# Counting ranks: column sums of compare tables on TensorE in place of later compares on VectorE

## The chip, the cores and the metric

The kernel runs on one core of a Trainium2 chip. The metric is the device time of one execution in microseconds, as the median of several runs. A hardware profile of one further execution gives the page and the trace that are read here. The engines are TensorE (PE, with its weight loads as PEld), VectorE (DVE), ScalarE (ACT), GpSimd (POOL) and SyncE (SP), which issues most of the DMAs. Each engine works through its own queue in order, and semaphores tie the queues together.

## What is computed

The program is a linear attention followed by a mixture-of-depths expert layer. For 4 batches, 8 heads, 768 positions and head size 64, the attention goes through blocks of 64 positions with a decaying state:

```python
for b in range(nb):
    intra = np.einsum('bhic,bhjc->bhij', qb, kb) * Dmask[None]
    intra = np.einsum('bhij,bhjd->bhid', intra, vb)
    inter = np.einsum('bhid,bhde->bhie', qb * lam_pow[None], kv_state)
    out[:, :, sl] = intra + inter
    kv_state = lam_block[None, :, None, None] * kv_state + np.einsum('bhsd,bhse->bhde', kb_dec, vb)
```

Its output, with heads side by side, is x of shape (4, 768, 512). In the second part each batch chooses the 128 positions with the highest gate score, and only these pass through a two-layer network:

```python
scores = np.einsum('bsd,d->bs', x, w_gate)
for b in range(B):
    top_idx = np.argpartition(-scores[b], capacity)[:capacity]
    xe = x[b, top_idx]
    ye = np.maximum(xe @ w1, 0.0) @ w2
    g = 1.0 / (1.0 + np.exp(-scores[b, top_idx]))
    out[b, top_idx] = x[b, top_idx] + g[:, None] * ye
```

## The kernel before

**Tiling and steps.** Positions are taken in groups of 128, two blocks of 64 each. A batch has NT = 6 groups, and the whole input NG = 24. The main loop has one step per group g. A step finishes group g and prepares the next ones: it multiplies masked scores by the values (`from_scores`, L356), copies the result out of PSUM to `x_b` on ScalarE (`outputs`, L370 and L372), starts the score products of group g+1 (`scores`, L285, and `from_states`, L345), masks them on VectorE (`masked`, L292), and for group g+2 computes the state products (`state_products`, L308), transposes queries and keys (`transposes`, L219 and L233, or `split_transposes`, L257, late in the run; ScalarE copies them to `qkT`), and decays queries on GpSimd (`queries_decayed`, L270). Keys are decayed on GpSimd (`keys_decayed`, L205). The state is advanced by `decay_state` on GpSimd (L318) and `next_state` on VectorE (L335), or by four folded operations on VectorE alone (L330).

**Order.** The schedule is manual: each engine gets its instructions in the order in which the Python calls are made. Steps below SPARE = 6 have one order, step SPARE has a mixture, and later steps have another. Work of the experts is put into later steps as numbered pieces (`put(step, key, piece)`, sorted by key by `in_order`), or into the dictionaries `front`, `early`, `gates`, `ranked` and `writes`.

**Ranks.** The gate score of each position is a product of `x_b` and the gate weights on VectorE (`gate_scores`, L395). To find the 128 best positions, the kernel counts for each position how many others beat it. One step after its group, `row` (L418) makes TensorE transpose the group's scores into a PSUM bank so that they lie along a row on every partition. ScalarE copies this to `sc_row` (L421), and VectorE compares it with the group's own scores, for ties (L424). `compare` (L434) then compares all scores of the groups up to this one with the group's own scores, one position per partition, and adds up the hits along the row into `beaten`. Comparing with groups that come later has to wait until these exist. `count_later` does that: in step t = 2, 4 and 5 of a batch (more of it in the last batch) it runs further compares (also L434) of older groups against newer parts of the row. `compare_older` takes a part of the last group's compare before the row is there. When a batch is counted, `ranks` adds the counts (L470) and builds a 0/1 table `hit` (L475). `tokens` multiplies it by position numbers on TensorE (`pk`, L486) and VectorE makes the list `tok` (L492, L495). With it GpSimd fetches the chosen rows (`xs`, L509). The expert transposes them (`pt`, L519), computes `ph` (L547) and `py` (L561), combines (`y`, L569), and GpSimd writes rows back (L577).

**Banks and loads.** Two PSUM banks, pm0 and pm1, are handed out in turn by `bank()` for `tq`, `tk`, `tqk`, `pb`, `pk`, `pt`; `ph` and `py` hold one over several steps. A bank's next user waits for the readers of the one before. The state products and, from step SPARE on, the transposed keys share one bank for each of the two blocks (`pu`). Loads of q, k and v go through pools of seven buffers, three loads are under way at a time, and the variable `ahead` says how many groups in advance they are asked for (4, then 3, then 5).

Of the kernel before, what the change touches and what calls it, by code (L numbers as in the profile page):

```python
# [9 lines left out]
BF16 = mybir.dt.bfloat16  # L10
I32 = mybir.dt.int32
AF = mybir.ActivationFunctionType
# [5 lines left out]
def kernel(  # L18
# [12 lines left out]
    nc = tc.nc  # L31
# [68 lines left out]
    def load_weights(i):  # L100
# [10 lines left out]
            src[j * 128 : (j + n) * 128, cols].rearrange("(c p) e -> p c e", p=128),  # L111
        )

    ident = const.tile([128, 128], FP32, name="ident")
    make_identity(nc, ident)

# [221 lines left out]
    def from_states(g):  # L338

        qs = qss.pop(g)  # L340
        for hp, hh, c in quarters():
            n = 2 * g + c
            if n % (2 * NT) == 0:
                continue
            nc.tensor.matmul(  # L345
                pos[g][half[hh ^ c], hh, 0, hp, :],
                lhsT=qs[half[hh], c, hp, :], rhs=states[n][half[hh], hp, :],
                start=(hp == 0), stop=False, skip_group_check=True,
            )
        for c in range(2):  # L350
            states.pop(2 * g + c, None)

    def from_scores(g):
        p, vn = ps_.pop(g), loaded.pop(g)[2]
# [47 lines left out]

        return out[0 : b + 1].flatten_outer_dims()

    rows_, beatens, toks, upto = {}, {}, {}, {}

    def row(g, pb=None):

        b, t = divmod(g, NT)
        if t == 0:  # L410
            rows_[b] = mod.tile([128, S], FP32, name="sc_row", tag="sc_row")
            beatens[b] = mod.tile([128, NT, NT + 1], FP32, name="beaten")
            nc.vector.memset(beatens[b][:], 0.0)
            upto[b] = {n: n for n in range(NT)}
        if pb is None:
            pb = bank([128, L], "pb")
        pb = pb[:, :L]
        nc.tensor.transpose(  # L418
            pb, in_=scs[b][:, t : t + 1].broadcast_to([128, 128]), identity=ident[:]
        )  # L420
# [3 lines left out]
        nc.vector.scalar_tensor_tensor(  # L424
            out=cmp[:, :L], in0=pb, scalar=scs[b][:, t : t + 1], in1=not_before[:],
            op0=ALU.is_equal, op1=ALU.mult, accum_out=beatens[b][:, t, NT : NT + 1],
        )

    def count(b, t, cols, op, at):
        cmp = mod.tile([128, S], BF16, name="cmp")
        nc.vector.tensor_scalar(  # L434
            out=cmp[:, : cols.stop - cols.start], in0=rows_[b][:, cols],
            scalar1=scs[b][:, t : t + 1], scalar2=None, op0=op, op1=ALU.add,
            accum_out=beatens[b][:, t, at : at + 1],
        )

    def count_later(b, groups, last):  # L440
        for t in groups:
            if upto[b][t] < last:
                cols = slice((upto[b][t] + 1) * L, (last + 1) * L)
                count(b, t, cols, ALU.is_gt, last)
                upto[b][t] = last

    def compare(g):
        b, t = divmod(g, NT)
        first = upto[b].pop(NT + t, 0)
        count(b, t, slice(first * L, (t + 1) * L), ALU.is_ge, t)  # L450
        if t == NT // 2 - 1 or t == NT - 1 or (b == B - 1 and t == NT - 2):
            count_later(b, range(t), t)
        elif t == NT - 2:
            count_later(b, range(NT // 3), t)

    def compare_older(g):

        b, t = divmod(g, NT)
        if t > 0:
            count(b, t, slice(0, t * L), ALU.is_ge, 0)  # L460
            upto[b][NT + t] = t

    def places(b):

# [125 lines left out]
    def put(step, key, piece):  # L590
        later.setdefault(step, []).append((key, piece))
# [5 lines left out]
    def plan(b):  # L597
        last = b == B - 1
        s = (b + 1) * NT
        ranks, tokens = places(b)  # L600
        if last:

            def last_row():
                compare_older(NG - 1)
                row(NG - 1, us[NG][1])
                compare(NG - 1)
                ranks()

            put(s, 35, last_row)
            put(s, 85, tokens)  # L610
        else:

            if b > 0:
                ranked[s + 1] = ranks
                if s + 8 <= NG:
                    put(s + 2, 1, tokens)
                else:
                    early.setdefault(s + 2, []).append(tokens)
            else:
                put(s, 1, ranks)  # L620
# [77 lines left out]
    for g in range(NG):  # L698
        if g == NT:
            for i, at in enumerate(weights_at):  # L700
                if at == g:
                    load_weights(i)
        ahead = 4 if g < NT - 1 else 3 if g < NT + 4 else 5
        while asked < min(g + ahead + 1, NG):
            load(asked)
            asked += 1
        if g != NT:
            for i, at in enumerate(weights_at):
                if at == g:
# [6 lines left out]
        if spare:  # L716
# [17 lines left out]
            state_products(g + 2)  # L734
            next_state(2 * g + 4)
            gate_scores(g)
            next_state(2 * g + 5, fold=True)
        else:
            lead = g > SPARE
            if g == SPARE:  # L740

                for r in rows:
                    row(r)
            if g + 2 < NG:
                if g <= FED:
                    keys_decayed(g + 2)
                decay_state(2 * g + 4)
            if FED <= g < NG - 3:
                keys_decayed(g + 3)
            from_scores(g)  # L750
            outputs(g)
            if g + 1 < NG:
                scores(g + 1)
                from_states(g + 1)
                if g == SPARE:
                    for r in rows:
                        compare(r)
                    in_order(pieces)
                masked(g + 1)
            if g % NT == 0 and lead and NGR:  # L760
                compare_older(g - 1)
            for piece in early.pop(g, []):
# [10 lines left out]
            if g in gates:  # L773
                gates.pop(g)()
            if g + 2 < NG:
                if g > SPARE + 1:
# [10 lines left out]
                in_order(pieces)  # L787
            if lead:
                for r in rows:
                    row(r, us[NG][0] if r == NG - 2 else None)  # L790
            if g + 2 < NG:
                next_state(2 * g + 5, fold=not lead)
            if lead:
# [43 lines left out]
```

## Time and profile before

The time before is 184.74 us (median of 3 runs, 183.54 to 185.18). The profiled execution has a span of 180.2 us.

| engine | busy us | share of the span | instructions |
|---|---|---|---|
| PE | 149.8 | 83% | 3586 |
| PEld | 119.5 | 66% | 3586 |
| DVE | 111.5 | 62% | 378 |
| ACT | 68.9 | 38% | 178 |
| POOL | 96.2 | 53% | 100 |

Busy time is an average over stages with different limits, so the chain of waits and the windows must say where an engine's time matters. A row of the page's groups reads: source line, engine, operation, output and inputs with shapes, count, busy time and mean duration of one, then the idle time of the engine just ahead of these instructions and what ended it. The DMA queues moved 31.99 MB in all and were nearly full until about 126 us.

### The profile page before, as it was taken

The numbers are of one execution on the slowest core, as the hardware profiler recorded it, in microseconds if no ns is written. First come the engines' busy times: TensorE is split into PE (matmuls) and PEld (weight loads), VectorE is DVE, ScalarE is ACT, GpSimd is POOL, SyncE is SP. The second block draws the span as 40 slices with busy tenths as digits, with TensorE's granted clock in tenths as the row PEclk, the third lists the DMA queues.
The fourth block names the chain that finished last, engine by engine and source line by source line (L and its number), as shares of the span: only waits on it lengthen the run. The fifth ranks groups of instructions, "written<-read, shape, count | busy, mean of one in ns | idle before, by whom it ended". The sixth has DMA issues, their size and how long they took to land.

```text
span 180.2 us, 8244 instructions
## 1 busy us (share of the span) xinstructions
PE 149.8 (83%) x3586; PEld 119.5 (66%) x3586; DVE 111.5 (62%) x378; ACT 68.9 (38%) x178; POOL 96.2 (53%) x100
## 2 busy tenths in 40 slices
PE   0799777776497999999977989989999997989980
PEld 0568666665386999776655668977666896459620
DVE  4814788899844445768996583589865779330010
ACT  2214555562144344644552552563343641011100
POOL 4358666945074665569786967867574600220002
PEclk9999999999859999999999999999999999999997
DMA  4999798999999998987999999989112131011001
GB/s 97 205 226 219 195 261 221 235 276 307 289 248 272 208 275 180 199 181 174 262 242 290 225 253 245 256 215 238 62 64 62 62 125 50 7 55 58 0 0 58
DMA packets 83381, 31.99 MB, mean 177 GB/s; under 512 B 75665, under 2 KB 79761, under 8 KB 83346
## 3 DMA queue, kind: packets, MB, share of 16 engines
q1 hardware_dynamic: 82560, 29.37, 67.8%
q0 software_dynamic: 640, 2.10, 3.4%
q8 instruction: 28, 0.46, 1.1%
q14 instruction: 7, 0.06, 0.1%
q10 hardware_dynamic: 146, 0.01, 0.0%
HBM read 24.12 MB, written 7.34 MB: 175 GB/s over the span
## 4 chain that ended last, share of the span: by engine, by line
PE 55%; issue 16%; DVE 14%; POOL 6%; DMA 4%; ACT 2%; POOLq 1%; ACTq 0%
PE py L561 10%; PE ph L547 9%; PE pu L308 6%; PE po L356 6%; PE po L345 5%; PE po L285 5%; DVE cmp L434 5%; PE tq L219 5%; POOL qs L270 2%; POOL decayed L318 2%; DMA qn<-in_q_dram 2%; DVE state L335 2%; DMA out_dram<-y,tok 2%; PE tqk L257 2%; DVE p L292 2%
## 5 line engine op out<-in xcount | busy, mean ns | idle before, releaser
L270 POOL TENSOR_TENSOR qs<-qkT,qpow 128x512 f32<-128x512 f32 x24 | 33.0, 1377 | 16.9 <-ACT qkT L224 9.5
L318 POOL TENSOR_TENSOR decayed<-state,decay 128x256 f32<-128x256 f32 x34 | 28.9, 849 | 23.1 <-DVE state L335 10.8
L547 PE MATMUL ph<-xsT,w_sb 128*128 128x128 f32 x256 | 31.1, 278 | 0.7 <-ACT xsT L523 0.7
L547 PEld LDWEIGHTS ph<-xsT,w_sb 128*128 128x128 f32 x256 | 29.5, 192 | 2.5 <-ACT qkT L264 1.2
L561 PE MATMUL py<-w_sb,hs 128*128 128x512 f32 x64 | 30.0, 602 | 0.1
L434 DVE TENSOR_SCALAR_CACHE_REDUCE cmp<-sc_row,sc 128x128 bf16<-128x128 f32 (+4 forms) x65 | 29.8, 503 | 0.0
L205 POOL TENSOR_TENSOR kd<-kn,kpow 128x512 f32<-128x512 f32 x24 | 25.8, 1074 | 4.9 <-DMA kn<-in_k_dram 4.9
L335 DVE TENSOR_TENSOR state<-pu,decayed 128x256 f32<-128x256 f32 x34 | 14.3, 422 | 16.3 <-ACT qkT L243 4.5
L395 DVE CUSTOM_DVE_ANT_0 xg<-x_b,wg_b 128x512 f32<-128x512 f32 x24 | 23.3, 969 | 0.0
L308 PE MATMUL pu<-vn,kd 64*64 64x64 f32 x704 | 19.3, 234 | 2.7 <-issue 1.2
L285 PE MATMUL po<-qkT 64*64 64x64 f32 x768 | 17.6, 227 | 4.1 <-issue 3.4
L292 DVE TENSOR_TENSOR p<-po,mask 128x512 f32<-128x512 f32 x24 | 16.5, 689 | 6.3 <-PE po L345 6.2
L308 PEld LDWEIGHTS pu<-vn,kd 64*64 64x64 f32 x704 | 16.4, 145 | 5.4 <-POOL kd L205 2.6
L356 PEld LDWEIGHTS po<-vn,p 64*64 64x64 f32 x768 | 14.3, 138 | 7.6 <-issue 5.7
L285 PEld LDWEIGHTS po<-qkT 64*64 64x64 f32 x768 | 15.1, 142 | 4.9 <-issue 3.8
L356 PE MATMUL po<-vn,p 64*64 64x64 f32 x768 | 17.8, 229 | 0.7 <-issue 0.7
L224 ACT COPY qkT<-tq 128x512 f32<-128x512 f32 x16 | 9.3, 584 | 23.2 <-PE tq L219 23.2
L561 PEld LDWEIGHTS py<-w_sb,hs 128*128 128x128 f32 x64 | 11.3, 191 | 10.0 <-issue 9.6
L372 ACT COPY x_b<-po 64x256 f32<-64x256 f32 x48 | 17.6, 366 | 0.6
L345 PE MATMUL po<-state,qs 64*64 64x64 f32 x704 | 17.2, 225 | 0.3 <-POOL qs L270 0.3
L219 PE MATMUL tq<-ident,qn 128*128 128x128 f32 x64 | 12.2, 322 | 5.1 <-DMA qn<-in_q_dram 5.1
L421 ACT COPY sc_row<-pb 128x128 f32<-128x128 f32 x22 | 5.9, 267 | 25.7 <-PE pb L418 25.6
(77 smaller groups left out, 182.7 us busy)
## 6 DMA issues: line engine op xcount, KB each, us to landing
qn<-in_q_dram SPq DMA_DIRECT2D x24, 256.0 KB, 4.6
kn<-in_k_dram SPq DMA_DIRECT2D x24, 256.0 KB, 4.4
vn<-in_v_dram SPq DMA_DIRECT2D x24, 256.0 KB, 4.8
out_dram<-x_b SPq DMA_DIRECT2D x18, 256.0 KB, 4.0
w_sb<-in_moe_w_dram SPq DMA_DIRECT2D x4, 512.0 KB, 5.7
w_sb<-in_moe_w_dram SPq DMA_DIRECT2D x8, 256.0 KB, 4.5
out_dram<-x_b SPq DMA_DIRECT2D x2, 768.0 KB, 6.4
xs<-out_dram,tok POOLq DMA_INDIRECT x4, 4.2
```

The lines of the kernel that those rows point to most:

```text
L205: nc.gpsimd.tensor_tensor(out=kd[:], in0=loaded[g][1][:], in1=kpow[:].rearrange("p a b -> p (a b)").unsqueeze(2).broadcast_to([128, H, D]) ...
L219: nc.tensor.transpose(tq[:, hp, :], in_=loaded[g][0][:, 2 * hp : 2 * hp + 2, :], identity=ident[:])
L270: nc.gpsimd.tensor_tensor(out=qs[:].rearrange("p c a i -> p c (a i)"), in0=qkTs[g][:, :, 0].rearrange("p c a i -> p c (a i)"), in1=qpow[:] ...
L285: nc.tensor.matmul(po[half[c], hh, 1, hp, :], lhsT=qkT[half[hh], c, 1, hp, :], rhs=qkT[half[hh], c, 0, hp, :], start=True, stop=True, skip ...
L308: nc.tensor.matmul(us[g][c][half[hh], hp * D : (hp + 1) * D], lhsT=kd[half[c], h, :], rhs=vn[half[c], h, :], start=True, stop=True, skip_g ...
L318: nc.gpsimd.tensor_tensor(out=t[:], in0=states[n][:], in1=decay[:], op=ALU.mult)
L345: nc.tensor.matmul(pos[g][half[hh ^ c], hh, 0, hp, :], lhsT=qs[half[hh], c, hp, :], rhs=states[n][half[hh], hp, :], start=(hp == 0), stop= ...
L356: nc.tensor.matmul(pos[g][half[hh ^ c], hh, 0, hp, :], lhsT=p[half[c], hh, hp, :], rhs=vn[half[c], 2 * hp + hh, :], start=(hp == 0 and (2 ...
L395: nc.vector.tensor_tensor_reduce(out=xg[:], in0=x_bs[b][:, t].rearrange("p a b e -> p (a b e)"), in1=wg_b[:], scale=1.0, scalar=0.0, op0=A ...
L434: nc.vector.tensor_scalar(out=cmp[:, : cols.stop - cols.start], in0=rows_[b][:, cols], scalar1=scs[b][:, t : t + 1], scalar2=None, op0=op, ...
L547: nc.tensor.matmul(ph[:, fc % 4, :], lhsT=w1_sb[:, dc, fc * 128 : (fc + 1) * 128], rhs=keep["xsT"][:, dc, :], start=(dc == 0), stop=(dc == ...
L561: nc.tensor.matmul(py[:], lhsT=keep["hs"][:, fc, :], rhs=w2_sb[:, fc, :], start=(fc == 0), stop=(fc == NFC - 1),)
```

## The change

The compare table of a group already holds, for each pair of a position in the group and an older position, whether the older one beats it or ties. Its sums along the row are the counts of the group's own positions. Its sums down the columns are what `count_later` computed anew: 128 less the column sum is the number of positions in the newer group that beat the older position. The change keeps each table (bf16, four buffers), and lets TensorE sum the columns, with the table as weights and a column of ones as the moving operand: one matmul of one column for each older group, t of them for group t (`column_sums`). ScalarE turns the sums into counts (`behind`: -1 times the sum plus 128) and writes them into `beaten`. `count_later` is dropped.

The sums of a table are issued in the step after it was made, in the bank of the next row (`pb`), directly behind the row's transpose and ahead of ScalarE's and VectorE's reads of that bank. The table of a batch's last group is left for the next step (`wait=1`) and summed in a bank of its own (`last_behind`), after which the ranks follow. Around this some orders change: in step 5 the older part of group 5's compare runs at the end in place of a folded state update, which moves behind the tokens of step 6; in step 7 the transposes come after the state products; tokens and fetch of batch 1 stand behind one expert piece; the last row is put one expert piece later, and its ranks behind it. Loads are asked for six groups ahead from step 13 on, and kept stores start one step later.

```diff
-    def count_later(b, groups, last):
-        for t in groups:
-            if upto[b][t] < last:
-                cols = slice((upto[b][t] + 1) * L, (last + 1) * L)
-                count(b, t, cols, ALU.is_gt, last)
-                upto[b][t] = last
+    def column_sums(b, t, cmp, pw):
+        for n in range(t):
+            nc.tensor.matmul(
+                pw[:, n : n + 1], lhsT=cmp[:, n * L : (n + 1) * L], rhs=ones_b[:],
+                start=True, stop=True,
+            )
+
+    def behind(b, t, cmp, pw):
+        nc.scalar.activation(
+            beatens[b][:, :t, t], pw[:, :t], AF.Copy, scale=-1.0, bias=float(L)
+        )
...
+        sums = []
+        for i in range(len(tables) - wait):
+            sums.append((*tables.pop(0), pb[:, L + i * NT : L + (i + 1) * NT]))
+            column_sums(*sums[-1])
-        nc.scalar.copy(out=rows_[b][:, t * L : (t + 1) * L], in_=pb)
+        nc.scalar.copy(out=rows_[b][:, t * L : (t + 1) * L], in_=pb[:, :L])
...
+        for args in sums:
+            behind(*args)
...
     def compare(g):
         b, t = divmod(g, NT)
-        first = upto[b].pop(NT + t, 0)
-        count(b, t, slice(first * L, (t + 1) * L), ALU.is_ge, t)
-        if t == NT // 2 - 1 or t == NT - 1 or (b == B - 1 and t == NT - 2):
-            count_later(b, range(t), t)
-        elif t == NT - 2:
-            count_later(b, range(NT // 3), t)
+        first = older.pop(g, 0)
+        table = count(b, t, slice(first * L, (t + 1) * L), t)
+        if t > 0 and not first:
+            tables.append((b, t, table))
...
+    def last_behind():
+        if not tables:
+            return
+        pw = bank([128, NT * NT], "pw")
+        sums = [(*a, pw[:, i * NT : (i + 1) * NT]) for i, a in enumerate(tables)]
+        tables.clear()
+        for args in sums:
+            column_sums(*args)
+        for args in sums:
+            behind(*args)
...
-                row(NG - 1, us[NG][1])
+                row(NG - 1, us[NG][1], wait=1)
                 compare(NG - 1)
+
+            def last_ranks():
+                last_behind()
                 ranks()
-            put(s, 35, last_row)
+            put(s, 45, last_row)
+            put(s, 55, last_ranks)
...
-                    put(s + 2, 1, tokens)
+                    put(s + 2, 15, tokens)
...
-                put(s + 2, 2, fetch)
+                put(s + 2, 16, fetch)
...
-        ahead = 4 if g < NT - 1 else 3 if g < NT + 4 else 5
+        ahead = 4 if g < NT - 1 else 3 if g < NT + 4 else 5 if g < FED else 6
...
-        if g >= 2 * NT - 1 and kept:
+        if g >= 2 * NT and kept:
             store_kept()
...
-            next_state(2 * g + 5, fold=True)
+            if g == SPARE - 1 and NGR:
+                compare_older(g)
+            else:
+                next_state(2 * g + 5, fold=True)
...
                 if g == SPARE:
-                    for r in rows:
-                        compare(r)
-                    in_order(pieces)
+                    in_order(pieces[:2])
+                    if NGR:
+                        next_state(2 * g + 3, fold=True)
+                    in_order(pieces[2:])
+                    if NGR:
+                        decay_state(2 * g + 4)
                 masked(g + 1)
+            if g in ranked:
+                last_behind()
...
-            if g <= SPARE + 1:
+            if g <= SPARE:
                 transposes(g + 2)
```

In step SPARE the row of group 5, its compare, `from_scores` and `last_behind` precede this block. In later steps `row` is called with `wait=1` when g is a multiple of NT.

More of the change, by code (lines that the diff above doesn't have):

```diff
@@ L112, in load_weights @@
         )
+    ones_b = const.tile([128, 1], BF16, name="ones_b")
+    nc.vector.memset(ones_b[:], 1.0)
     ident = const.tile([128, 128], FP32, name="ident")
@@ L350, in from_states @@
         for c in range(2):
-            states.pop(2 * g + c, None)
+            states.pop(2 * (g - 1) + c, None)
     def from_scores(g):
@@ L403, in rows_upto, with row @@
         return out[0 : b + 1].flatten_outer_dims()
-    rows_, beatens, toks, upto = {}, {}, {}, {}
-    def row(g, pb=None):
+    rows_, beatens, toks, tables, older = {}, {}, {}, [], {}
+    def row(g, pb=None, wait=0):
         b, t = divmod(g, NT)
@@ L413, in row @@
             nc.vector.memset(beatens[b][:], 0.0)
-            upto[b] = {n: n for n in range(NT)}
         if pb is None:
-            pb = bank([128, L], "pb")
-        pb = pb[:, :L]
+            pb = bank([128, L + NT * NT], "pb")
         nc.tensor.transpose(
-            pb, in_=scs[b][:, t : t + 1].broadcast_to([128, 128]), identity=ident[:]
+            pb[:, :L], in_=scs[b][:, t : t + 1].broadcast_to([128, 128]), identity=ident[:]
         )
-        nc.scalar.copy(out=rows_[b][:, t * L : (t + 1) * L], in_=pb)
+        sums = []
@@ L423, in row @@
+        for i in range(len(tables) - wait):
+            sums.append((*tables.pop(0), pb[:, L + i * NT : L + (i + 1) * NT]))
+            column_sums(*sums[-1])
+        nc.scalar.copy(out=rows_[b][:, t * L : (t + 1) * L], in_=pb[:, :L])
         cmp = mod.tile([128, S], BF16, name="cmp")
         nc.vector.scalar_tensor_tensor(
-            out=cmp[:, :L], in0=pb, scalar=scs[b][:, t : t + 1], in1=not_before[:],
+            out=cmp[:, :L], in0=pb[:, :L], scalar=scs[b][:, t : t + 1], in1=not_before[:],
@@ L426, in row, with count @@
             op0=ALU.is_equal, op1=ALU.mult, accum_out=beatens[b][:, t, NT : NT + 1],
         )
-    def count(b, t, cols, op, at):
-        cmp = mod.tile([128, S], BF16, name="cmp")
+        for args in sums:
+            behind(*args)
+    def count(b, t, cols, at):
+        cmp = mod.tile([128, S], BF16, name="table", bufs=4)
         nc.vector.tensor_scalar(
             out=cmp[:, : cols.stop - cols.start], in0=rows_[b][:, cols],
-            scalar1=scs[b][:, t : t + 1], scalar2=None, op0=op, op1=ALU.add,
+            scalar1=scs[b][:, t : t + 1], scalar2=None, op0=ALU.is_ge, op1=ALU.add,
@@ L437, in count @@
             accum_out=beatens[b][:, t, at : at + 1],
         )
-    def count_later(b, groups, last):
-        for t in groups:
-            if upto[b][t] < last:
-                cols = slice((upto[b][t] + 1) * L, (last + 1) * L)
-                count(b, t, cols, ALU.is_gt, last)
-                upto[b][t] = last
+        return cmp
+    def column_sums(b, t, cmp, pw):
[4 more added lines that the diff above has]
+            )
@@ L459, in compare_older @@
         if t > 0:
-            count(b, t, slice(0, t * L), ALU.is_ge, 0)
-            upto[b][NT + t] = t
+            tables.append((b, t, count(b, t, slice(0, t * L), 0)))
+            older[g] = t
+    def last_behind():
[8 more added lines that the diff above has]
+            behind(*args)
     def places(b):
@@ L742 @@
                 for r in rows:
-                    row(r)
+                    row(r, wait=1)
+                for r in rows:
+                    compare(r)
             if g + 2 < NG:
@@ L746 @@
                     keys_decayed(g + 2)
-                decay_state(2 * g + 4)
+                if lead or not NGR:
+                    decay_state(2 * g + 4)
             if FED <= g < NG - 3:
@@ L750 @@
             from_scores(g)
+            if g == SPARE and NGR:
+                last_behind()
             outputs(g)
@@ L755 @@
                 if g == SPARE:
-                    for r in rows:
-                        compare(r)
-                    in_order(pieces)
+                    in_order(pieces[:2])
[3 more added lines that the diff above has]
+                    if NGR:
+                        decay_state(2 * g + 4)
                 masked(g + 1)
+            if g in ranked:
+                last_behind()
             if g % NT == 0 and lead and NGR:
@@ L775 @@
             if g + 2 < NG:
-                if g > SPARE + 1:
+                if g > SPARE:
                     transposes(g + 2)
@@ L789 @@
                 for r in rows:
-                    row(r, us[NG][0] if r == NG - 2 else None)
+                    row(r, us[NG][0] if r == NG - 2 else None, wait=g % NT == 0)
             if g + 2 < NG:
```

## The prediction

> **What bounds the kernel now.** I read the page first, then the chain of waits in order of time, then the timeline of each engine around the counting, then windows.
>
> ```profile
> span 180.2 us, 8244 instructions
> PE 149.8 (83%) x3586; PEld 119.5 (66%) x3586; DVE 111.5 (62%) x378; ACT 68.9 (38%) x178; POOL 96.2 (53%) x100
> ...
> PEclk9999999999859999999999999999999999999997
> ...
> L434 DVE TENSOR_SCALAR_CACHE_REDUCE cmp<-sc_row,sc 128x128 bf16<-128x128 f32 (+4 forms) x65 | 29.8, 503 | 0.0
> ```
>
> TensorE (PE) is the fullest engine, and has one dip of its clock, near 46 to 54 us. Counting (L434) is the largest VectorE job, but VectorE as a whole has a third of the span free, so removing counts pays only where the chain runs through them. The chain shows where:
>
> ```profile
> 44.57 2.68 DVE cmp L434 x12
> ...
> 47.27 0.21 DVE rank L470
> ...
> 47.50 0.97 DVE hit L475
> ...
> 48.52 0.32 PE pk L486 x6
> 48.84 0.95 PE tq L219 x4
> ```
>
> At batch 0's end everything is behind six compares. Windows of the same place (PE busy first, granted clock third from the end):
>
> ```profile
> 45.10:48.50 3.40, 0.81 (x40) 0.67 (x40) 3.29 (x14) 0.58 (x2) 0.04 (x1) 0.92 1.15 322
> 48.50:51.90 3.40, 3.17 (x44) 2.80 (x48) 0.91 (x3) 1.15 (x3) 2.35 (x2) 0.50 0.98 204
> ```
>
> TensorE works 0.81 us of 3.4, and then runs at half clock. Last, TensorE's timeline at the tail, where the bracket is idle time and what ended it:
>
> ```profile
> 146.48 2.94 PE L547 MATMUL ph<-xsT,w_sb 128*128 128x128 f32 x24
> 150.48 0.29 PE L418 MATMUL pu<-ident,sc 128*128 128x128 f32 x1 [1.05 <-DVE sc L395]
> ...
> 154.97 0.29 PE L486 MATMUL pk<-ids,hit 128*128 128x2 bf16 x6
> ```
>
> The last row waits 1.05 us for a score that stood behind compares on VectorE. Elsewhere (58 to 77 us, 111 to 131 us) TensorE is simply full.
>
> [...] The trace's nearest row, six pk matmuls of 2 columns with bf16 weights, takes 0.29 us with the last one's own 0.164: (0.29-0.164)/5 = 25 ns. [...] The trace has 204 ns for the 128x1 exponential and one table load in all. [...] `decayed` takes 0.73 us alone and 1.18 us beside the score product L395, and kd stays at 1.03 beside compares. So fewer compares do not make GpSimd faster.
>
> **The change part by part.**
>
> *Counts removed.* 38 later counts go; batch 0's last count of 768 becomes 640 + 128. By the starts in VectorE's timeline one costs 0.27 us (128 columns), 0.40 (256), 0.53 (384). Where it matters:
> - Step 3 (about 31 us): two counts, 0.67 us, ahead of the mask product; that would then wait for TensorE instead, 0.2 us earlier: **-0.2**.
> - Step 6: five later counts plus the long count go (1.8 + 0.9 us). In exchange the 640 table runs before the row. From the row's score at 43.49: table until 44.37, row compare and 128 table until 45.1, both ScalarE subtractions by about 45.3, rank and hit until 46.45. pk stands behind L345 on TensorE, which ended 47.15 and now has nine sums ahead (9 x 0.027 = 0.24): pk at 47.4 against 48.52. But the folded state update (four L330, 0.85 us) is moved behind the tokens, and the key transposes L233 need its bank: tokens 48.0, fold 48.9, L233 at 48.95 against 49.79: **-0.8**, not -1.1. Queued behind L233 are the next state products and step 7. GpSimd has `decayed` behind the fetch now; it ends near 50.0, before the keys of group 8 are copied, so it is hidden.
> - Steps 8 to 11, and 15 to 18: counts lie beside full TensorE work or GpSimd's chain (qs 1.27, decayed 1.18, kd 1.03): nothing. Step 18 alone ends a 0.08 us wait.
> - Steps 13 and 19: 1.7 to 2 us of counts go, but the next state L335 waits for ScalarE's key copy (91.46 and 126.67 us) and rank follows it in order, as before: nothing.
> - Tail: three 256 counts and one 128 go ahead of the last score (1.47 us), so the score is ready near 149.0; the row is moved one hidden chunk later (key 45), 150.1. TensorE's 1.05 us of idle becomes work. Seven sums ahead of the row's readers and five in the next bank take 12 x 0.027 = 0.32: **-0.7**. Rank waits for a subtraction queued behind the ReLU (about 152.6), hit ends near 153.9, pk is reached near 154.1: not a new wait.
>
> *Column sums added.* 60 matmuls of one column with 60 weight loads. Bounds: 27 ns (pk, with its step to the next instruction)[...]. I take 27, since weights and operands have pk's form. Those not counted above: 6 in steps 3 to 5, which are serial from score to score (**+0.15**); 6 in steps 9 to 11 and 4 in step 12, of which about half are idle time's (**+0.1**); 10 in steps 15 to 18 (**+0.25**); 5 in step 13 hide under the wait for L335 at 89.5; 5 in step 19, 1 in step 21, 2 in step 22 (**+0.2**).
>
> *Subtractions added.* 20 ACTIVATEs of about 0.2 us. Each waits for the row's compare on VectorE, and the x_b copies are queued behind it on ScalarE; these waited for L424 nine times already (3.5 us), so only the 0.2 is new. ScalarE then idles 0.9 us or more before the next qkT copy in most steps: hidden, except in step 13, where x_b and the next transposes' bank come later: **+0.15**.
>
> *Order.* In step 14 py precedes pk, so the 0.78 us wait of pk for the qkT copy L264 lies under py (0.97); the row then waits for the token reduction behind pk (98.7 against 99.15): **-0.45**. Batch 1's rank bank in step 19 adds **+0.1**. The first compare of step 6 and the transposes of step 7 change places with waits already there.
>
> *Loads.* Six groups ahead only starts after step 12, and stores kept back start one step later. The one GpSimd wait for kn there (1.80 us at 106.87) ends while TensorE is full: nothing.
>
> Sum without the clock: -0.2 - 0.8 - 0.7 + 0.15 + 0.1 + 0.25 + 0.2 + 0.15 - 0.45 + 0.1 - 0.08 = **-1.3 us**.
>
> *Clock.* In the window 45.1 to 48.5 TensorE would work about 1.7 to 1.9 us instead of 0.81 (pk and tq move in, sums are added). The window before it (41.7 to 45.1) has about 1.95 and is granted full clock. If it stays full, the run of tq, L233, L308, L356, L285, L345 from 48.8 costs 3.1 us (its lengths in step 8) instead of 5.6; GpSimd's qs of group 8 (about 51.5) and the landing of the fetched rows (48.2 + 4.2) stop the gain at about 1.5: **-1.5 us**.
>
> **The rivals.**
> - *Forecast*: counts leave three places and the clock holds: 184.74 - 1.3 - 1.5 = 181.9, say **182.0**. For: the idle of 1.37 us before pk is what empties the window. Against: the 1.48 us gap within L285 (44.8 to 46.3), put down to "issue", is not touched and may grow.
> - *Clock falls anyway*: 184.74 - 1.3 = **183.4**.
> - *Hidden*: chains move to the qkT copies and GpSimd, and only the tail is gained: 184.74 - 0.7 + 0.5 of sums = **184.5**. For: two of three batch ends show that.
> - *Slower*: [...] For: they stand on TensorE, the bound, in front of the row's readers. Against: pk's 25 ns.
>
> **How the numbers follow.** Forecast 0.48, clock falls 0.28, hidden 0.10, slower 0.14. Faster by over 1% means below 182.9: the first, and a quarter of the second: 0.55. Slower than 186.6 or close to it: 0.14. The rest, 0.31, within 1%. The range leaves out the slower rival and the fastest tail (sums for nothing and L285's gap gone): 180.6 to 185.3.
>
> **What would show it.** Right: 28 compare instructions; pk of batch 0 near 47.4 and full clock in 48 to 54 us; no idle before the last row; sums some 27 ns apart. Wrong: a clock dip still there, long starts between sums, TensorE idle for L330 longer than 0.5 us in step 6, x_b copies or the row's readers turning up as releasers of PE waits.

## The result, and the profile after

The changed kernel takes 193.49 us (median of 4 runs, 192.5 to 196.88), the kernel before 184.14 us beside it (182.87 to 185.18). The ratio is 1.049, with a 95% interval of 1.041 to 1.057. A second measurement on another occasion gave 193.55 us and 1.053 (1.044 to 1.063). Medians take in all executions, while ratios leave out those more than 1.5% above the fastest of their kernel, such as the profiled one (196.88 us). A second profile of the changed kernel, with a span of 190.9 us (e15 below), shows the same long wait.

The lines of the page of after that answer to those of before:

```profile
span 195.2 us, 8295 instructions
PE 158.3 (81%) x3646; PEld 127.7 (65%) x3646; DVE 100.2 (51%) x305; ACT 70.8 (36%) x198; POOL 95.0 (49%) x100
...
PEclk9999999999579889999988975799999999999997
...
L441 DVE TENSOR_SCALAR_CACHE_REDUCE table<-sc_row,sc 128x128 bf16<-128x128 f32 (+4 forms) x28 | 16.9, 607 | 0.1
```

The counting did what it was made for: 28 compares in place of 65, and VectorE is busy 11.3 us less. Yet the span grew. The known dip of the clock near slice 11 is still there, and a long one has come, in slices 24 to 26 (112 to 127 us, 0.5 to 0.7), besides two shallow ones (0.8 in slices 14, 15, 21 and 22). So the loss is sought in the second half. The starts of the product of masked scores and values (`from_scores`) mark the steps. Step 16 runs from 108.1 to 125.5 us, 17.4 us, against 8.0 us before (103.7 to 111.7). In the second profile it takes 16.3 us. These 8 to 9 us are nearly the whole difference of the medians (9.35). Step 8 is longer as well, 9.9 us against 5.8, but 5.8 in the second profile.

The chain of waits of after in that step (start, length, what):

```profile
105.30 0.95 SPq L384
...
106.30 5.93 DMA out_dram<-x_b
...
112.38 0.99 POOL xs L533
113.39 0.74 POOL decayed L320
...
114.16 0.42 DVE state L337
```

and the timeline of the same stretch, with idle time and its cause in the bracket:

```profile
112.38 0.99 POOL L533 DMA_INDIRECT xs<-out_dram,tok  x1 [7.78 <-DMA out_dram<-x_b]
...
114.16 0.42 DVE L337 TENSOR_TENSOR state<-pu,decayed 128x256 f32<-128x256 f32 x1 [7.51 <-POOL decayed L320]
...
116.38 1.13 PE L347 MATMUL po<-state,qs 64*64 64x64 f32 x32 [7.14 <-POOL qs L272]
```

The chain now leads through stores. Batch 1's outputs are not stored group by group: they are kept, and written by two "kept stores" of three groups each (768 KB, `store_kept`). The second of them is issued at 105.30. Right behind it, at 106.30, goes the store of group 13, and the views above name that one. But the wait in GpSimd's queue that belongs to the fetch is another line (durations in ns, then its start in us):

```profile
L533 POOLq EVENT_SEMAPHORE  x1: 8204/8204/8204, 103.4 to 103.4; - x1
```

It waits for the semaphores of the two kept stores, and it ends at 111.63, when the second one has landed (111.60). GpSimd's fetch of batch 1's chosen rows reads what these stores write. It starts 0.75 us later, after GpSimd has idled for 7.78 us. Behind the fetch stand `decayed`, `kd` and `qs` in GpSimd's queue, and they started after it, one behind the other (113.39, 114.07 and 115.07). The next state waits for `decayed` (7.51), TensorE for `qs` (7.14). After this TensorE runs at a lower clock: 0.64 in the window from 112 to 120 us and 0.72 from 120 to 128 (half clock from 114.28 to 124.52).

Why is the store so late? SyncE's timeline before, from the first kept store to the second (`out_dram<-x_b` is a store, x2 two of them in a row, the kept one first), with GpSimd's fetch below:

```profile
84.78 2.06 SPq L382 DMA_DIRECT2D out_dram<-x_b  x1
86.89 0.48 SPq L67 DMA_DIRECT2D qn<-in_q_dram  x1
88.18 0.64 SPq L67 DMA_DIRECT2D kn<-in_k_dram  x1
88.91 1.91 SPq L67 DMA_DIRECT2D vn<-in_v_dram  x1
90.88 3.09 SPq L382 DMA_DIRECT2D out_dram<-x_b  x2
...
100.44 0.99 POOL L509 DMA_INDIRECT xs<-out_dram,tok  x1
```

and after:

```profile
93.46 0.37 SPq L67 DMA_DIRECT2D qn<-in_q_dram  x1
96.61 0.37 SPq L67 DMA_DIRECT2D kn<-in_k_dram  x1
97.42 0.37 SPq L67 DMA_DIRECT2D vn<-in_v_dram  x1
97.83 2.12 SPq L384 DMA_DIRECT2D out_dram<-x_b  x2
100.00 0.98 SPq L67 DMA_DIRECT2D qn<-in_q_dram  x1
101.08 1.36 SPq L67 DMA_DIRECT2D kn<-in_k_dram  x1
102.54 2.71 SPq L67 DMA_DIRECT2D vn<-in_v_dram  x1
105.30 1.48 SPq L384 DMA_DIRECT2D out_dram<-x_b  x2
```

Before, the second kept store leaves at 90.88. It takes 6.46 us from issue to landing there, so it lands at 97.34, some 3 us ahead of the fetch, which waits for nothing. After, it leaves at 105.30, though the last of its data (group 11) was copied by ScalarE before 83 us. Count the loads in front of it from group 17 on. Before there is one group: 17 in step 12, then the store. After there are three: in step 12 the number ahead goes from five to six, so that groups 17 and 18 are asked for at once, ahead of that step's stores; and the store belongs to step 13 now, where group 19 is asked for first. Each of these groups takes SyncE 4.2 to 5.3 us in after (89.28, 93.46 and 100.00 are their first issues), since in groups 17 and 18 a load is held until an earlier one has landed (2.7 us ahead of the `kn` at 96.61), while in group 19 the three issues themselves take 5.0 us, for a reason that isn't shown. A store whose data has long been there stands behind three groups of loads.

### The profile page after: what moved, and what is told of

Its sections match the earlier page's. It is cut to its first block, busy times and chain, and to the rows that moved or that the text cites. A ratio compares the mean times of both kernels' runs of the same rounds, so it can differ in the third digit from the quotient of the medians.

```text
span 195.2 us, 8295 instructions
## 1 busy us (share of the span) xinstructions
PE 158.3 (81%) x3646; PEld 127.7 (65%) x3646; DVE 100.2 (51%) x305; ACT 70.8 (36%) x198; POOL 95.0 (49%) x100
## 4 chain that ended last, share of the span: by engine, by line
PE 56%; issue 15%; DVE 10%; DMA 7%; POOL 5%; ACT 4%; POOLq 1%; SPq 1%; ACTq 0%; DVEq 0%
PE ph L571 13%; PE py L585 8%; PE pu L310 6%; PE po L358 6%; PE po L287 5%; PE tq L221 5%; PE po L347 5%; DVE xg L397 3%; DMA out_dram<-x_b 3%; PE tqk L259 2%; DMA qn<-in_q_dram 2%; ACT qkT L226 2%; POOL decayed L320 2%; DVE state L337 2%; PE pb L419 2%
## 5 line engine op out<-in xcount | busy, mean ns | idle before, releaser
L320 POOL TENSOR_TENSOR decayed<-state,decay 128x256 f32<-128x256 f32 x34 | 28.4, 837 | 21.0 <-DVE state L337 11.6
L571 PE MATMUL ph<-xsT,w_sb 128*128 128x128 f32 x256 | 34.7, 297 | 0.7 <-ACT xsT L547 0.7
L571 PEld LDWEIGHTS ph<-xsT,w_sb 128*128 128x128 f32 x256 | 32.9, 210 | 1.5 <-ACT xsT L547 1.1
L585 PE MATMUL py<-w_sb,hs 128*128 128x512 f32 x64 | 31.1, 619 | 0.6 <-ACT hs L576 0.6
L337 DVE TENSOR_TENSOR state<-pu,decayed 128x256 f32<-128x256 f32 x34 | 14.4, 422 | 28.7 <-POOL decayed L320 12.1
L347 PE MATMUL po<-state,qs 64*64 64x64 f32 x704 | 17.9, 230 | 8.4 <-POOL qs L272 7.4
L397 DVE CUSTOM_DVE_ANT_0 xg<-x_b,wg_b 128x512 f32<-128x512 f32 x24 | 24.2, 1007 | 0.0
L310 PE MATMUL pu<-vn,kd 64*64 64x64 f32 x704 | 19.6, 237 | 5.1 <-issue 2.5
L287 PE MATMUL po<-qkT 64*64 64x64 f32 x768 | 18.0, 228 | 5.1 <-issue 4.4
L310 PEld LDWEIGHTS pu<-vn,kd 64*64 64x64 f32 x704 | 16.8, 148 | 7.7 <-issue 3.1
L347 PEld LDWEIGHTS po<-state,qs 64*64 64x64 f32 x704 | 15.3, 145 | 9.2 <-POOL qs L272 7.7
L287 PEld LDWEIGHTS po<-qkT 64*64 64x64 f32 x768 | 15.2, 142 | 6.1 <-issue 4.9
L585 PEld LDWEIGHTS py<-w_sb,hs 128*128 128x128 f32 x64 | 11.4, 194 | 10.5 <-issue 9.6
L358 PE MATMUL po<-vn,p 64*64 64x64 f32 x768 | 17.5, 228 | 0.0
L358 PEld LDWEIGHTS po<-vn,p 64*64 64x64 f32 x768 | 14.1, 138 | 4.6 <-issue 2.9
L441 DVE TENSOR_SCALAR_CACHE_REDUCE table<-sc_row,sc 128x128 bf16<-128x128 f32 (+4 forms) x28 | 16.9, 607 | 0.1
L533 POOL DMA_INDIRECT xs<-out_dram,tok x4 | 4.1, 1020 | 26.2 <-DVE tok L519 18.3
```

What stands on the lines that cost most here:

```text
L287: nc.tensor.matmul(po[half[c], hh, 1, hp, :], lhsT=qkT[half[hh], c, 1, hp, :], rhs=qkT[half[hh], c, 0, hp, :], start=True, stop=True, skip ...
L310: nc.tensor.matmul(us[g][c][half[hh], hp * D : (hp + 1) * D], lhsT=kd[half[c], h, :], rhs=vn[half[c], h, :], start=True, stop=True, skip_g ...
L337: nc.vector.tensor_tensor(out=new[:], in0=u, in1=decayed.pop(n)[:], op=ALU.add)
L347: nc.tensor.matmul(pos[g][half[hh ^ c], hh, 0, hp, :], lhsT=qs[half[hh], c, hp, :], rhs=states[n][half[hh], hp, :], start=(hp == 0), stop= ...
L358: nc.tensor.matmul(pos[g][half[hh ^ c], hh, 0, hp, :], lhsT=p[half[c], hh, hp, :], rhs=vn[half[c], 2 * hp + hh, :], start=(hp == 0 and (2 ...
L397: nc.vector.tensor_tensor_reduce(out=xg[:], in0=x_bs[b][:, t].rearrange("p a b e -> p (a b e)"), in1=wg_b[:], scale=1.0, scalar=0.0, op0=A ...
```

## The experiments

Theory S: what costs is the place of the second kept store behind the loads. Rivals: L, that six groups ahead cost by themselves; and that the counting costs. Each ratio is to the kernel before in the same measurement. The second kept store's issue is from each run's profile, and so is the wait: GpSimd's idle time before the fetch, where the fetch's own semaphore wait ends with that store's landing.

| run | counting | groups ahead | kept stores | load groups from 17 on in front of the second | second store issued, us | fetch waits for it, us | median us | ratio (95%) |
|---|---|---|---|---|---|---|---|---|
| after | new | 6 | steps 12, 13, behind loads | 3 | 105.30 | 7.78 | 193.49 | 1.049 (1.041-1.057) |
| e5 | old | 6 | 12, 13, behind | 3 | 99.28 | 4.89 | 190.94 | 1.044 (1.039-1.050) |
| e8 | new | 6 | 12, 13, ahead | 2 | 98.71 | 4.02 | 188.9 | 1.031 (1.022-1.040) |
| e1 | new | 6 | 11, 12, behind | 2 | 98.55 | 2.85 | 188.11 | 1.025 (1.015-1.036) |
| e2 | new | 5 | 12, 13, behind | 2 | 98.66 | 4.16 | 188.02 | 1.024 (1.013-1.035) |
| e4 | old | 5 | 12, 13, behind | 2 | 96.10 | none | 186.85 | 1.021 (1.008-1.035) |
| e6 | old | 6 | 11, 12, behind | 2 | 97.29 | 1.23 | 185.07 | 1.010 (1.005-1.014) |
| e3 | new | 5 | 11, 12, behind | 1 | 94.66 | none | 185.75 | 1.006 (means of 2 and 5 runs, no interval) |
| e9 | new | 6 | 11, 12, ahead | 0 | 88.47 | none | 185.99 | 1.003 (0.999-1.006) |

The ratios go with the number of load groups in front of the second store: over 1.04 with three, 1.01 to 1.03 with two, about 1.01 or less with one or none. They go broadly with the wait too, except for e4.

**Undoing either edit (e1, e2), both (e3), and the late store in the kernel before (e4).**

```diff
 e1, e3: -        if g >= 2 * NT and kept:
         +        if g >= 2 * NT - 1 and kept:
 e2, e3: -        ... else 5 if g < FED else 6
         +        ... else 5
 e4 (kernel before): the first of these edits the other way round
```

> The changed kernel with the kept stores of batch 1 starting one step earlier again, as before the change; all else as changed (loads six ahead). Theory S (late store: the fetch of batch 1's rows waits 7.8 us for the store of the same rows, GpSimd's decay and VectorE's state stand behind it, and TensorE idles 7.1 us and then runs cold): about 184, between 183 and 186. Rival C (the column sums and the subtractions cost the time on TensorE and ScalarE): stays above 191. Rival L (loads six ahead crowd the DMA queues and put the store behind them): falls only in part, 187 to 191.

> The changed kernel with loads five groups ahead again; the kept stores stay one step late. Theory S: the second kept store is still issued a step late, so the fetch still waits, though two loads fewer stand ahead of it: 189 to 193. Rival L: falls to about 184 to 186. Rival C: unchanged, above 192.

> The changed kernel with stores and loads both as before, so that only the counting and its orders are changed. Theory S with my pricing of the counting: 182 to 184 (1.3 us or more below before). Rival C: above 191. If the counting gains nothing: 184 to 185.

> The kernel before, with only the start of the kept stores moved one step later. Theory S: the fetch of batch 1's rows waits here too, the time rises by 4 to 9 us to 188 to 193. Rivals C and L: within 1% of before.

Either edit undone wins back some 5 us of the 9, and both undone about 8. So the loss belongs to the two together, not to one of them, and what e1 kept (188.1) spoke for rival L at first. But e1 has the same wait in a hidden form: its fetch starts at 105.43 after 2.85 us of idle time that the trace puts down to a mask product long done. The fetch's own semaphore wait shows the cause:

```profile
L533 POOLq EVENT_SEMAPHORE  x1: 4463/4463/4463, 100.2 to 100.2; - x1
```

It waits for the two kept stores and ends at 104.68. The second was issued at 98.55 and landed at 104.65. The time of e2 (188.0) lies below what S had given it and above what L had. In e4 the store landed at 101.70, while GpSimd was busy until 102.46, so the fetch did not wait in the profile. That profile is of the shortest of its four executions, 185.31 us. Whether the longer ones waited isn't known. So S isn't shown to explain e4's 2%; they stay open.

**The two edits without the counting (e5), six ahead alone (e6), and the store ahead of the loads (e8, e9).**

```diff
 e5, e6: the kernel before with
-        ahead = 4 if g < NT - 1 else 3 if g < NT + 4 else 5
+        ahead = 4 if g < NT - 1 else 3 if g < NT + 4 else 5 if g < FED else 6
 e5 too: -        if g >= 2 * NT - 1 and kept:
         +        if g >= 2 * NT and kept:
 e8: the changed kernel with
+        if g >= 2 * NT and kept:
+            store_kept()
         while asked < min(g + ahead + 1, NG):
...
-        if g >= 2 * NT and kept:
-            store_kept()
 e9: as e8, with g >= 2 * NT - 1
```

> The kernel before with both load-and-store edits (the kept stores from step 12 on, six groups ahead from step 12 on) and the old counting. Theory S, the second kept store is issued behind the loads and GpSimd's fetch of batch 1 waits for it: the whole loss comes along without the new counting, 190 to 194 us, and the fetch waits 5 us or more for the store. Rival R, the loss needs the new counting as well (its later fetch, its column sums, its table reads): about the sum of the two edits tried alone, 186 to 188.5 us.

> The kernel before with six groups ahead from step 12 on alone; the kept stores stay at steps 11 and 12. Theory S: two more loads stand ahead of the second store at most, and the fetch waits for it 0 to 3 us: 184 to 187.5 us, and whatever is lost is lost between the starts of steps 16 and 18. Rival L, six groups ahead cost by themselves (transfers in the way of everything): 187 to 190 us, spread over steps 12 to 20, without a wait on the store.

> The changed kernel with one statement moved: a step's kept store is issued ahead of that step's loads, not behind them; the store is as late as in the changed kernel and the loads still go six ahead. Theory S, what costs is the place of the store behind the loads in SyncE's queue: the fetch of batch 1 waits under 2 us for the store, and the time falls to 184 to 188 us. Rival L, six groups ahead or the late step as such cost: 190 to 194 us, as with the changed kernel.

> The changed kernel, six ahead, with the kept stores at steps 11 and 12, each issued ahead of its step's loads, so that no load of group 17 or 18 stands in front of the second one. Theory S, only the place of the second kept store in SyncE's queue costs: it is issued before 91 us, the fetch of batch 1 doesn't wait for it, and the time is that of the new counting with five ahead, 184.5 to 186.5 us. Rival L, six groups ahead cost by themselves what the store's place doesn't explain: 187 to 189 us without a wait on the store.

e5 takes the loss into the kernel before, with no column sum in it: 190.94 us, 7.3 us above its neighbour (183.62), most of the changed kernel's 9.4. The counting isn't the cause of that part. In e6, where S had allowed for a wait of 0 to 3 us, the fetch's semaphore wait ends at 102.49 and the second kept store landed at 102.46; GpSimd had idled 1.23 us when the fetch started. e8 missed its number (188.9 instead of 184 to 188), and its timeline shows why:

```profile
85.96 1.06 SPq L384 DMA_DIRECT2D out_dram<-x_b  x1
...
94.28 0.37 SPq L67 DMA_DIRECT2D qn<-in_q_dram  x1
95.11 0.37 SPq L67 DMA_DIRECT2D kn<-in_k_dram  x1
95.84 1.83 SPq L67 DMA_DIRECT2D vn<-in_v_dram  x1
97.71 1.42 SPq L384 DMA_DIRECT2D out_dram<-x_b  x2
...
105.36 0.99 POOL L533 DMA_INDIRECT xs<-out_dram,tok  x1 [4.02 <-DMA out_dram<-x_b]
```

The first kept store is ahead of step 12's loads now, at 85.96, but the second belongs to step 13 and still stands behind both groups of step 12. Of the pair at 97.71 the first is the store of group 12, and the kept one is the second, as the chain of waits has it:

```profile
98.71 5.86 DMA out_dram<-x_b
```

It was the place in the queue that mattered here, not the place in a step. In e9 no load of group 17 or 18 stands in front of it any more:

```profile
82.00 2.12 SPq L384 DMA_DIRECT2D out_dram<-x_b  x1
88.47 2.10 SPq L384 DMA_DIRECT2D out_dram<-x_b  x1
...
104.93 0.99 POOL L533 DMA_INDIRECT xs<-out_dram,tok  x1 [0.15 <-issue]
```

The wait is gone, and the changed kernel, with all its counting and all its loads, is level with the kernel before.

**The same move in the kernel before (e11).** 

```diff
+        if g >= 2 * NT - 1 and kept:
+            store_kept()
         ahead = 4 if g < NT - 1 else 3 if g < NT + 4 else 5
...
-        if g >= 2 * NT - 1 and kept:
-            store_kept()
```

> The kernel before with one statement moved: a kept store is issued ahead of its step's loads. Theory S: the second kept store is issued some us earlier, but the fetch of batch 1 waited for nothing of it in the kernel before, so 183 to 184.5 us, no difference. Rival: transfers of 1.5 MB come earlier and lie beside others, loads of groups 16 and 17 later: 185 us or more.

185.85 us against 184.77, a ratio of 1.005 (1.001 to 1.008). Where the fetch didn't wait there was nothing to gain, and about half a per cent was lost: S missed its 183 to 184.5 us, and the rival's "185 us or more" came out. So stores ahead of the loads are not free. The rival's reason, transfers that get in each other's way, was not tested.

**The counting by itself (e3, e7, e10, e12).** With loads and stores as before, the new counting ought to have given the forecast's -1.3 us. e3 gave none; its 185.75 us lie above both of the ranges set down for it without rival C. In the last step its lines are the same as in after (TensorE's timeline of after):

```profile
161.00 3.84 PE L571 MATMUL ph<-xsT,w_sb 128*128 128x128 f32 x32
164.67 0.27 PE L419 MATMUL pu<-ident,sc 128*128 128x128 f32 x1
164.78 0.32 PE L450 MATMUL pu<-ones_b,table 128*128 128x1 bf16 x7
164.96 1.14 PE L571 MATMUL ph<-xsT,w_sb 128*128 128x128 f32 x8
165.93 0.27 PE L450 MATMUL pw<-ones_b,table 128*128 128x1 bf16 x5
166.78 2.84 PE L585 MATMUL py<-w_sb,hs 128*128 128x512 f32 x6 [0.58 <-ACT hs L576]
```

The row (L419) waits for nothing now, as forecast. But py waits 0.58 us for the second ReLU: the last sums (`pw`) took the free one of the two banks, and py got the bank that the ReLU still reads. e7 puts `pw` into the bank of row 22, which is read no more:

```diff
-        pw = bank([128, NT * NT], "pw")
+        pw = us[NG][0][:, 256 : 256 + NT * NT]      (in the last step)
```

> The new counting alone (loads and stores as before), and the last column sums written to a free part of the bank of row 22 in place of a bank of the rotating pool. Theory T, the gain at the end was eaten because the last sums took the free bank, so that py had to wait for the second ReLU: py's wait of 0.58 us in the last step goes, the last stretch is 0.5 to 0.7 us shorter than with the new counting alone (34.4 us), and the time is about 185 us. Rival: the wait stays, since the bank isn't its cause, and the time is that of the new counting alone, 185.7 us.

```profile
156.20 0.27 PE L450 MATMUL pu<-ones_b,table 128*128 128x1 bf16 x5
156.33 2.82 PE L586 MATMUL py<-w_sb,hs 128*128 128x512 f32 x6
```

The wait is gone, and py starts 1.39 us after the last row (156.33 - 154.94) instead of 2.11 in e3: 0.7 us, as theory T has it. From the start of the last product of masked scores and values to the end it is 33.7 us, against 34.3 before and 34.4 in e3. The whole is none the shorter, 186.27 us and 1.011 (1.000 to 1.021). Two more runs looked for what eats the gains. e10 keeps column sums for batch 0 alone, with the old compares and their order for the others; e12 puts tokens and fetch back to their old keys (15 and 16 become 1 and 2). All three have loads and stores as before.

> Loads and stores as before; column sums of tables for batch 0 alone (steps 1 to 7), the old counting with its order for batches 1 to 3. Theory G, the new counting gains about 1 us in steps 6 and 7 and gives it back in later steps (step 14 +0.5, step 19 +0.3, step 20 +0.3, by the lengths of steps): 182 to 183.5 us, 0 to 1 us under the kernel before. Rival N, what steps 6 and 7 gain is lost in the clock and in gaps of TensorE right after: 183.5 to 186 us, as with the new counting in all batches.

> The new counting alone (loads and stores as before), with the list of the tokens and the fetch of batches 1 and 2 back at the head of step 14's and step 20's expert work (py behind pk again). If the new order of py and pk gives what it was meant to: step 14 gets longer by about 0.5 us, and the time is 186 to 186.5 us. If the later fetch is what the new counting loses: step 16 is shorter or the same, and the time is 184 to 185 us.

e10: 184.78 us, 1.002 (0.999 to 1.006). e12: 188.24 us, 1.010 (1.002 to 1.018), by its ratio no different from e7. e10 lies within the range of N and at the very edge of G's, which had it 0 to 1 us under the kernel before. e12 met neither of its two ranges and decides nothing.

**Everything mended, with five and with six groups ahead, and the changed kernel beside them (e13, e14, e15).** e13 has the new counting, five ahead, the stores of e9 and the bank of e7; e14 is the same with six ahead; e15 is the changed kernel.

> The new counting with five groups ahead, the kept stores at steps 11 and 12 ahead of the loads, and the last column sums in the bank of row 22. If the counting is worth what steps 6 and 7 (about -1 us) and the last step (-0.7 us) show, less what steps 14, 19 and 20 cost (+1 us): 0.5 to 1 us under the kernel before, a ratio of 0.994 to 0.997. If those gains are lost in gaps and clock elsewhere: a ratio of 1.000 to 1.012.

> The same with six groups ahead from step 12 on, which is the changed kernel with the place of the stores and the last bank mended. Theory S: no more than 0.5 us from the run with five ahead. Rival L, six ahead cost by themselves: 1.5 us or more above it.

> The changed kernel as it is, beside the two mended ones on the same chip: 192 to 195 us, and the fetch of batch 1 waits 6 to 9 us for the second kept store. If the store's place weren't the cause but the chip of the first measurement, it would be 185 to 188 us here.

e13: 185.14 us against 184.02, ratio 0.998 (0.995 to 1.002), e14: 184.86 us, 1.005 (1.002 to 1.009), e15: 193.55 us, 1.053. The list of waits of e15:

```profile
POOL xs L533 <- DMA out_dram<-x_b: 8.0, 1, 8.0
```

So the place of the stores and one bank are worth some 4.8% (1.053 to 1.005), and the counting, with the stores ahead of the loads, nothing that can be measured: e13 lies between the two ranges set down for it. Why e7 and e12, with the stores behind the loads as in the kernel before, are 1% above it stays open, since their fetches did not wait for a store. Whether the sixth group costs anything by itself is not settled. By the ratios it is 0.7% (1.005 to 0.998), more than S and less than L had given it. But the medians of e14 and e13 stand the other way round, and e6's 1.0% in the kernel before holds a wait for the store. No version tried is measurably faster than the kernel before.

## Why the prediction was wrong

**The step that failed** is "Loads. Six groups ahead only starts after step 12, and stores kept back start one step later ... nothing". I looked at what waits for a load, and found one wait that was hidden. I didn't ask who reads the stores: the fetch of batch 1 reads the output that they write, with some 3 us to spare. Nor did I follow SyncE's queue, in which two groups of loads for one step come to stand ahead of the store. The term was 0 and measured +9 us; e5 has most of it without the counting, e9 is rid of it with the counting. None of the rivals held it either, since all of them were about counting. It started one step earlier than I wrote, too, there and in the section on the change: the sixth group is first asked for in step 12.

**Step 6 (-0.8): right in its sum.** From the row's transpose to the key transposes it is 5.36 us in after (44.94 to 50.30) and was 6.24 (43.55 to 49.79): -0.9. pk waits for `hit` no more (1.37 before). That the sum fits is partly luck. From the row on, pk comes 0.8 us earlier, not the 1.1 of the forecast; the gap within the score products is 0.2 us longer than before. The fold behind the tokens, priced at 0.3, held nothing up. The chain of after:

```profile
44.94 0.32 PE pb L419
...
46.45 1.70 issue
48.16 0.52 PE po L287 x18
...
49.20 0.24 PE pk L510 x6
49.44 0.86 PE tq L221 x4
50.30 0.82 PE pu L235 x3
```

**Clock holds (-1.5): wrong in this execution, and not in the counting's hands.** The windows of after at the same place (clock third from the end):

```profile
45.10:48.50 3.40, 1.70 (x71) 1.48 (x73) 2.40 (x8) 1.53 (x6) 0.00 (x0) 1.00 1.05 328
48.50:51.90 3.40, 3.06 (x64) 2.30 (x55) 1.68 (x7) 1.14 (x3) 1.75 (x2) 0.64 1.10 253
```

TensorE's activity is as I worked it out (1.70 us, forecast 1.7 to 1.9), and the clock still falls. Within L287 there is a gap of 1.70 us without a cause in the trace, the one that I named as the risk. In e13 it is 1.15 us, TensorE is busy 2.25 us in that window, and the clock stays whole:

```profile
44.30:47.70 3.40, 2.25 (x106) 2.03 (x104) 2.39 (x8) 1.54 (x6) 0.00 (x0) 1.00 1.07 370
47.70:51.10 3.40, 2.68 (x82) 2.07 (x71) 1.77 (x8) 1.14 (x3) 2.32 (x3) 1.00 1.01 227
```

It is no rule by the gap alone: e10 has 1.15 us there too, and its clock falls. Nor do these runs show one by activity, as I took it. In the 3.40 us ahead of the fall TensorE was busy 1.11 us before (44.55 to 47.95) and 1.70 us in after (46.03 to 49.43), while a window of 1.77 us in after (41.70 to 45.10) kept its clock, as the one of before at the same place did (1.88; the forecast has 1.95). The forecast's 1.7 to 1.9 spans both cases, so a window of about 1.9 that kept its clock was no proof. Of the twelve profiles with column sums in batch 0 two have no such fall: in e8 and e13 31 products of L347 in a row take 0.64 us, at 51.51 and 52.54. The ten others and the five without column sums have it: there a run of 31 or 32 of them (L345 in the old kernel) takes 1.07 to 1.17 us. So a dip that comes in nearly every execution can't be booked as gained because one of its causes goes.

**Tail (-0.7): the idle time went, as worked out, and came back as py's wait of 0.58 us.** I followed the row's bank, but not the next one: `pw` takes a turn in a rotation of two, and shifts who gets which bank. e7 shows the -0.7.

**Sums at 27 ns: right.** Seven sums take 0.32 us, one 0.17: (0.32 - 0.17)/6 = 25 ns. The slower rival (186.6 us) rested on a higher price of a sum that no trace shows; it ended on the right side for the wrong reason.

**Later steps: a little too low.** In e3, where loads and stores are as before, steps 19 to 22 take 22.75 us together (21.80 before): +0.95 where I had +0.3. Step 14 is 6.7 us (7.0), -0.3 for -0.45, since the next state's wait on VectorE (1.85 us before L310, in e3 as in after) took over from pk's.

**The sum of the counting (-1.3)** isn't found. Its gains can be seen in steps 6 and 7, and in the last step once the bank is mended; with both, e13 is at 0.998. What takes them away is not settled. One profile of each can't tell: step 16, 8.0 us before, takes 9.9 in e7, 10.4 in e13 and 11.2 in e10, but 7.7 in e3, and 11.4 in e11, which has the old counting. TensorE's gaps without a cause sum to 4.9 to 13.6 us in the profiles taken, more than the effect that is sought.

## What to carry to other kernels

Before an in-order queue gets a longer lookahead or a later store, write down what stands in it in order, what each entry waits for, and who reads what each store writes: a store that needed nothing was as late here as what stood ahead of it (14.4 us later: 105.30 in place of 90.88). Two edits that cost 1.0 to 2.5% each by themselves made 4.4 to 4.9% together; both push the same store past the slack of the same reader. An extra user of a rotating pair of buffers changes the buffer of every later user; follow the rotation to the next long hold.

## What the runs showed of the hardware

- The gate product `xg` (L397 on VectorE, 128x512) takes 0.69 us in the median of after. Once its fetch was away, GpSimd ran `decayed`, `kd`, `qs` and `kd` in a row, from 113.39 to 117.32 us. One `xg` started at 114.50, beside the last three, and took 3.38 us (1.49 at most before), while these three took 1.04, 1.26 and 1.03, none longer than elsewhere. In the chain of after this `xg` stands with 3.30 us, behind the wait for the fetch. In e8 the same three came after the fetch as well (1.04, 1.26 and 1.03 us), and one `xg` has 3.30 us of the chain there again.
- TensorE stopped within runs of matmuls that wait for nothing in the trace: 1.48 us within the score products of step 6 before, 0 to 2.03 us there in the other runs. In e14, where it was short there (0.33 us), one of 2.07 us came later, in the products of masked scores and values (L358), below (bracket: idle time). Its cause is open.

```profile
45.77 0.52 PE L287 MATMUL po<-qkT 64*64 64x64 f32 x21 [0.33 <-issue]
...
52.26 0.38 PE L358 MATMUL po<-vn,p 64*64 64x64 f32 x4 [2.07 <-issue]
```
